# A planned attention and MLP kernel: new durations for the planner, and the order of its work searched anew

## The chip, the cores and the metric

The kernel runs on one core of one Trainium2 chip. The metric is the device time of one execution in microseconds, the median of three runs. Of a core's engines, five matter here: TensorE (PE in the profile, with its weight loads as a row of their own, PEld), VectorE (DVE), ScalarE (ACT), GpSimd (POOL), and SyncE (SP), which here only issues DMAs. Each engine works through its own instructions in a fixed order and waits at semaphores for the others.

## The reference

Four layers on one sequence of 2048 tokens of width 448, in bfloat16. An attention layer with 16 heads of 28 and an MLP with squared ReLU alternate twice, with the same weights both times.

```
def _A_ref(x, wqkv, wo):                 # H = 16, Dh = 28
    qkv = (x @ wqkv).reshape(B, S, 3, H, Dh) ...
    scores = jnp.einsum("bhqd,bhkd->bhqk", q, k) * Dh ** -0.5
    p = _softmax(scores, axis=-1)
    o = jnp.einsum("bhqk,bhkd->bhqd", p, v)
    return o.transpose(0, 2, 1, 3).reshape(B, S, D) @ wo

def _B_ref(x, w1, b1, w2, b2):           # F = 1792
    r = relu(x @ w1 + b1)
    return (r * r) @ w2 + b2

x = x + _A_ref(_layernorm(x), A_wqkv, A_wo)
x = x + _B_ref(_layernorm(x), B_w1, B_b1, B_w2, B_b2)
x = x + _A_ref(_layernorm(x), A_wqkv, A_wo)
x = x + _B_ref(_layernorm(x), B_w1, B_b1, B_w2, B_b2)
```

The softmax takes the exponential of 2 x 16 x 2048 x 2048 scores. Spread over 128 partitions this is 2048 units of 128x512 scores.

## The kernel before, in words

**Tiles.** The queries of a layer are cut into blocks of 256 (the last two of the second layer of 128), the heads into four groups of four, the keys into 16 blocks of 128. A *unit* is one head of one query block against as many key blocks as fill 128x512. TensorE computes scores as keys times queries with contraction over 32 rows, so that several heads run in different rows of the array side by side.

**Score groups.** `s_stream` takes three units at a time, the *score group*, into a tile `sc` of three PSUM banks; there are two such tiles. There are 683 groups. `e_stream` gives each group one exponential on ScalarE (L994), 1536 wide, into a tile `pt` (11 buffers). In some groups ScalarE takes only two of the units, 1024 wide, and VectorE the third: `a_unit` and `a_rest` compute its exponential in three VectorE passes (L1059 from PSUM, L1076, and L1090, which writes the result) and one GpSimd pass (L1083) between the last two. Which groups give a unit away is decided in `apart`: group numbers in `FORCE` do so, those in `SKIP` do not, and the others do it if VectorE's load and backlog in the plan are below limits (`BUSY`, `TB` and others).

**The other work.** `p_stream` multiplies the exponentials with the values (L1153, tile `oT`), which also gives the denominators. `norm_pair` and `norm_turn` divide. `chain` carries a query block through the output projection, the layer norm (statistics at L537 and L542, the inverse root on GpSimd, `xn` at L647, transposes on TensorE at L587, their copy `xnT` at L599), the MLP (matmuls at L684, ReLU at L1349 on VectorE or L1347 on ScalarE, square at L1356 or L1354, additions to `x` at L1289) and, in the first layer, the keys, values and queries of the second. All of this runs on TensorE and VectorE between the score groups. TensorE gets filler work as well: a score group can be computed several times over (up to `MORE` more times) and `heat` issues matmuls whose result nobody reads (L1407).

**The order.** There is no scheduler at run time. `Planner` simulates all engines while the kernel is built: every `Op` has an engine, a duration in microseconds, dependencies, and buffers to acquire; the planner repeatedly takes the operation that can start first (by priority where several can) and emits its instructions. `LAT` and `PAIR` are the delays that the plan assumes between the end of an operation on one engine and the start of one on another. `PACE` maps score-group numbers to settings of the planner's constants from there on. So a change of a duration or a constant changes no instruction's work, only which instructions are emitted (who computes a unit, filler) and their order on each engine.

Of the kernel before, what the change touches and what calls it, by code (L numbers as in the profile page):

```python
# [118 lines left out]
CUTS = (0, 10, 16)  # L119
CH = 4.0  # L120
QP = 8.0
FORCE = (26, 42, 46, 57, 59, 85, 86, 102, 105, 106, 107, 170, 171, 332, 335, 410, 413, 462, 466, 561, 563, 565, 567,
        576, 583, 584, 597, 598)
SKIP = (12, 13, 16, 18, 21, 22, 25, 29, 44, 47, 87, 151, 153, 154, 155, 168, 331, 333, 334, 372, 373, 375, 377, 412,
        559, 560, 562, 581, 595)
PACE = {
    0: {'ASIDE': 2.0, 'BUSY': 0.97, 'CH': 4.0, 'CHUNK': 1, 'C_PRIO': 1.6, 'EV': 2.9, 'FAR': 9, 'HOLD': 6,
         'KEEP': 6, 'L0N': 7.0, 'L1N': 5.6, 'LAG': 12, 'LASTP': 3.2, 'LEAD': 15, 'LOW': 0.85, 'MARGIN': 1.5,
         'MORE': 1, 'NEAR': 6, 'PRE': 0.5, 'QP': 8.0, 'SLACK': 0.5, 'SOON': 0, 'SPAN': 15, 'TB': 1.8, 'V_AGE':
         6, 'V_LAST': 1.8, 'V_LATE': 4.6, 'V_PRIO': 8.5, 'V_WAIT': 5},  # L130
    6: {'V_LATE': 3.5, 'C_PRIO': 2.6},
    12: {'HOLD': 4, 'KEEP': 2, 'V_LATE': 5.2},
    18: {'CHUNK': 3, 'V_LAST': 3},
    36: {'CHUNK': 2},
    54: {'QP': 5},
    60: {'V_AGE': 4},
    66: {'V_AGE': 5},
    84: {'BUSY': 0.995},
    90: {'NEAR': 8, 'BUSY': 0.97},
    96: {'NEAR': 6, 'BUSY': 0.995},  # L140
    114: {'NEAR': 8},
    150: {'LAG': 5, 'CH': 5, 'SOON': 0.5},
    156: {'MARGIN': 2.5, 'L0N': 6.0},
    162: {'TB': 2.2, 'KEEP': 5},
    174: {'KEEP': 2, 'HOLD': 5, 'LAG': 8},
    192: {'MORE': 2},
    198: {'MORE': 1, 'FAR': 12},
    204: {'NEAR': 6, 'EV': 1.5, 'PRE': -0.3},
    210: {'NEAR': 8, 'EV': 2.9, 'PRE': 0.5},
    216: {'KEEP': 3, 'V_WAIT': 3.5},  # L150
    240: {'LAG': 16, 'LASTP': 2.6, 'SPAN': 11},
    246: {'LAG': 8, 'LASTP': 3.2, 'SPAN': 15, 'MORE': 2, 'V_WAIT': 2.5},
    252: {'V_LATE': 4.0},
    282: {'MORE': 1},
    288: {'MORE': 2},
    306: {'CHUNK': 3},
    318: {'CHUNK': 2},
    360: {'ASIDE': 1.0, 'HOLD': 4},
    366: {'V_AGE': 3, 'L1N': 5.8},
    402: {'L1N': 5.0, 'CHUNK': 1, 'HOLD': 6},  # L160
    414: {'L1N': 5.8},
    426: {'HOLD': 5, 'SPAN': 20},
    432: {'LOW': 0.9},
    444: {'V_PRIO': 2.8},
    450: {'V_PRIO': 8.5},
    522: {'HOLD': 6, 'V_LATE': 4.6},
    528: {'HOLD': 5, 'V_LATE': 4.0},
    534: {'PRE': 0.8, 'L0N': 7.8, 'LOW': 0.95},
    540: {'ASIDE': 0.3, 'SPAN': 11},
    552: {'LAG': 5},  # L170
    576: {'FAR': 17},
    582: {'FAR': 12},
    588: {'FAR': 17, 'V_LAST': 3.5, 'SLACK': 0.2},
    594: {'V_LAST': 3, 'SLACK': 0.5},
    648: {'KEEP': 2, 'CHUNK': 2, 'LEAD': 12},
}


# [12 lines left out]
class Op:  # L191
    __slots__ = ("eng", "dur", "fn", "deps", "acq", "rel", "mode", "sets", "start", "end", "res", "turn", "ready", "lat", "need", "got", "more", "room", "port", "durs")

    def __init__(self, eng, dur, fn, deps=(), acq=None, rel=None, mode="full", sets=(), lat=0.0, need=1, port=False):
# [7 lines left out]
        self.need, self.got, self.more, self.port = need, [], 0.0, port  # L202


LAT = {"PE": 0.25, "ACT": 0.28, "DVE": 0.07, "POOL": 0.10, "DMA": 2.0, "-": 0.0}
PAIR = {("PE", "ACT"): 0.275, ("PE", "DVE"): 0.197, ("DVE", "ACT"): 0.1, ("DVE", "POOL"): 0.1, ("DVE", "DVE"): 0.035,
        ("POOL", "DVE"): 0.035, ("PE", "PE"): 0.0, ("ACT", "ACT"): 0.0, ("POOL", "POOL"): 0.0}


# [99 lines left out]
def kernel(  # L309
# [593 lines left out]
    def s_stream():  # L903
        while at[0] < len(units):
            gi = len(gbuf)
            globals().update(PACE.get(gi, {}))
            js = ahead(3)
            us = [units[j] for j in js]
            gbuf.append({"n": len(us)})

            def fn(e, gi=gi, us=us, js=js):
                sc = ps_sc.tile([P, 3 * 512], DT.float32, name="sc", tag="sc")
                gbuf[gi]["sc"] = sc
                dst = [sc[:, k * 512:k * 512 + 512] for k in range(len(us))]
                ks = list(range(len(us)))

                def next_at(j):
                    at[0] = j
                    rest = ahead(1)
                    at[0] = rest[0] if rest else len(units)  # L920
                    return rest
                own, j = True, None
                if OWN3 and bank_free(o.start) and next_at(js[-1] + 1):
                    j = apart(at[0], o.start, us)
                if j is None and len(us) == 3 and THIRD:
                    own = False
                    next_at(js[1] + 1)
                    j = apart(at[0], o.start, us[:2], 0.0)
                if j is None:
                    next_at(js[-1] + 1)  # L930
                else:
                    if not own:
                        us, ks = us[:2], ks[:2]
                        gbuf[gi]["n"] = 2
                    us, ks = us + [units[j]], ks + [3]
                    taken.add(j)
                    gbuf[gi]["in"] = not own and units[j][0] == us[0][0]
                    held[0] += not gbuf[gi]["in"]
# [12 lines left out]
                for k, (pi, kb, r, hh) in zip(ks, us):  # L951
                    where.setdefault((pi, kb), []).append((gi, k, hh))
                    if len(where[pi, kb]) == G:
                        pl.tok["u", pi, kb] = o

                short = (HOT if len(units) - at[0] > ENDU else HOTE) - pl.load(HWIN)
                again = 0
                if short > 0 and gi > 0:
                    last = ("e" in gbuf[gi - 1] and gbuf[gi - 1]["e"].end) or pl.clock["ACT"] + 1.35
                    again = max(0, min(MORE, int(min(o.room, last - LAT["PE"] - 0.05 - o.end) / 0.22)))  # L960
                o.more = 0.22 * again
                for i in list(range(4)) * (again + 1):
                    for k, (pi, kb, r, hh) in enumerate(us):
                        if i >= r:
                            continue
                        l, qb, g, *_ = passes[pi]
                        t0, nt = blocks[l][qb]
                        rows = slice(DHP * hh, DHP * hh + DHP)
                        nc.tensor.matmul(dst[k][:, i * nt * P:(i + 1) * nt * P],  # L969
                                         lhsT=K_sb[l][rows, g, (kb + i) * P:(kb + i + 1) * P],  # L970
                                         rhs=Q_sb[rows, g, t0 * P:(t0 + nt) * P],
                                         start=True, stop=True, tile_position=(DHP * hh, 0))
            o = gbuf[gi]["s"] = Op("PE", 0.227, fn,
                                   deps=list({d for u in us for d in needs(u)}), acq=R_sc, mode="row", sets=("s", gi))
            yield o
        s_left.clear()
        pl.tok["send"] = o
# [7 lines left out]
    def e_stream():  # L985
        gi = 0
        while gi < len(gbuf) or s_left:
            yield Op("-", 0.0, None, deps=[("s", gi)])
            n = gbuf[gi]["n"] * 512

            def fn(e, gi=gi, n=n):
                e_now[:] = [e_now[0] + n // 512 + ("x" in gbuf[gi]), gi]
                pt = gbuf[gi]["pt"] = ptp.tile([P, 3 * 512], DT.bfloat16, name="pt")
                t = nc.scalar.activation(out=pt[:, 0:n], in_=gbuf[gi]["sc"][:, 0:n], func=AF.Exp,  # L994
                                         scale=float(np.log(2.0)) * 2.0 ** -FRAC)
                if gbuf[gi].get("x") is gbuf[gi]["s"]:
                    apart_from(gi, t)
            o = gbuf[gi]["e"] = Op("ACT", n / 1200 + 0.051, fn, deps=[("s", gi)], acq=R_pt, need=n // 512 + gbuf[gi].get("in", 0),
                                   rel=gbuf[gi]["s"], sets=("e", gi))
            yield o  # L1000
            gi += 1
# [456 lines left out]
```

## Time and profile before

| | |
|---|---|
| median of three runs | 845.28 us (845.02 to 845.38) |
| the profiled execution's own time | 845.39 us |
| span of its trace | 843.3 us |
| busy PE / DVE / ACT / POOL | 805.7 / 788.5 / 827.2 / 210.3 us |
| exponentials on ScalarE, 1536 and 1024 wide | 445 and 238 |
| units on VectorE (L1059) | 237 |
| score matmuls (L969) | 5120 |
| filler matmuls of `heat` (L1407) | 133 |
| granted TensorE clock | 1.000 |

The busy time of an engine is the union of its instructions' intervals. Instructions of one engine overlap (the next one starts before the last has written its result), so the mean time of one instruction is longer than the step from one to the next.

### The profile page before, as it was taken

How to read it: one execution, taken by the hardware profiler on the slowest of the kernel's cores; microseconds unless marked ns; L12 is line 12 of the kernel's file. 1: busy time of each engine (PE TensorE's matmuls, PEld its weight loads, DVE VectorE, ACT ScalarE, POOL GpSimd, SP SyncE). 2: the span in 40 equal slices, each digit the busy share in tenths (PEclk: the TensorE clock that was granted, in tenths of full speed). 3: DMA queues.
4: the chain of work that ended last, by engine and by line, in shares of the span. 5: the costliest groups of instructions: out<-in, count | busy, mean ns of one | idle time of the engine just before them, and what ended most of it. 6: DMA issues, size and time to landing. Idle time of an engine off the chain costs nothing.

```text
span 843.3 us, 28075 instructions
## 1 busy us (share of the span) xinstructions
PE 805.7 (96%) x12089; PEld 422.3 (50%) x12089; DVE 788.5 (93%) x1531; ACT 827.2 (98%) x698; POOL 210.3 (25%) x332
## 2 busy tenths in 40 slices
PE   8999999999999999999999999999999999999997
PEld 4455544454544545455445444434455454545665
DVE  7999999999999999999999999999999998989954
ACT  8999999999999999999999999999999999999994
POOL 3211322322222223322222223322212223121200
PEclk9999999999999999999999999999999999999999
DMA  9200100000000000000000000011100001000000
GB/s 244 74 3 2 26 22 12 15 15 16 8 9 16 15 15 16 15 3 15 2 3 2 2 2 3 15 29 29 32 9 14 26 15 31 21 13 15 14 20 13
DMA packets 32312, 17.94 MB, mean 21 GB/s; under 512 B 17786, under 2 KB 31739, under 8 KB 32188
## 3 DMA queue, kind: packets, MB, share of 16 engines
q1 hardware_dynamic: 32188, 16.16, 7.0%
q8 instruction: 94, 1.54, 0.8%
q14 instruction: 30, 0.25, 0.1%
HBM read 13.87 MB, written 2.06 MB: 19 GB/s over the span
## 4 chain that ended last, share of the span: by engine, by line
ACT 43%; PE 33%; DVE 15%; issue 8%; POOL 1%; DMA 0%; ACTq 0%; DVEq 0%; POOLq 0%
ACT pt L994 43%; PE mt L684 13%; PE sc L969 11%; PE oT L1153 6%; DVE r L1349 2%; DVE v_i L1059 2%; DVE v_e L1076 1%; DVE pt L1090 1%; PE mt L1407 1%; PE sc L684 1%; PE tp L587 1%; DVE K_sb L1076 1%; DVE st L537 1%; DVE x_sb L1289 1%; DVE K_sb L1059 1%
## 5 line engine op out<-in xcount | busy, mean ns | idle before, releaser
L994 ACT ACTIVATE pt<-sc 128x1536 bf16<-128x1536 f32 (+1 forms) x683 | 816.9, 1464 | 1.7 <-PE sc L969 1.4
L969 PE MATMUL sc<-Q_sb,K_sb 32*128 32x256 bf16 (+1 forms) x5120 | 301.0, 265 | 27.7 <-ACT pt L994 20.7
L969 PEld LDWEIGHTS <-K_sb 32*128 32x128 bf16 x5120 | 128.6, 92 | 209.1 <-issue 160.7
L1083 POOL TENSOR_SCALAR v_i<-v_i 128x512 int32<-128x512 int16 x126 | 89.2, 708 | 291.8 <-DVE v_e L1076 290.2
L1153 PE MATMUL oT<-pt,V_sb 128*32 128x256 bf16 (+1 forms) x4098 | 157.0, 268 | 0.8 <-ACT pt L994 0.5
L684 PE MATMUL mt<-xnT,w 128*128 128x256 bf16 (+1 forms) x928 | 121.9, 269 | 0.6 <-DVE r L1349 0.3
L1153 PEld LDWEIGHTS <-V_sb 128*32 128x32 bf16 x4352 | 89.3, 96 | 52.9 <-issue 49.6
L684 PEld LDWEIGHTS <-w 128*128 128x128 bf16 x952 | 77.6, 98 | 36.4 <-issue 28.6
L1059 DVE TENSOR_SCALAR v_i<-sc 128x512 int32<-128x512 f32 x126 | 85.7, 682 | 5.2 <-PE sc L969 4.5
L1076 DVE SCALAR_TENSOR_TENSOR v_e<-v_i 128x512 f32<-128x512 uint16 x126 | 87.6, 699 | 0.3
L1083 POOL TENSOR_SCALAR K_sb<-K_sb 128x512 int32<-128x512 int16 x64 | 45.3, 708 | 138.6 <-DVE K_sb L1076 134.5
L1349 DVE TENSOR_SCALAR r<-mt 128x512 bf16<-128x512 f32 x108 | 73.7, 682 | 5.4 <-PE mt L684 4.7
L684 PE MATMUL mt<-w,V_sb 128*128 128x448 bf16 (+1 forms) x274 | 68.3, 352 | 0.0
L1083 POOL TENSOR_SCALAR V_sb<-V_sb 128x512 int32<-128x512 int16 x47 | 34.3, 729 | 101.6 <-DVE V_sb L1076 100.7
L1059 DVE TENSOR_SCALAR K_sb<-sc 128x512 int32<-128x512 f32 x64 | 43.7, 683 | 1.9 <-PE sc L969 1.6
L1289 DVE TENSOR_TENSOR x_sb<-x_sb,mt 128x448 bf16<-128x448 bf16 (+1 forms) x61 | 37.0, 607 | 8.9 <-PE mt L684 8.5
L1407 PE MATMUL mt<-xn,ident 128*128 128x448 bf16 x133 | 44.2, 355 | 1.1 <-DVE x_sb L1289 0.3
L1076 DVE SCALAR_TENSOR_TENSOR K_sb<-K_sb 128x512 f32<-128x512 uint16 x64 | 44.1, 694 | 0.1
L1090 DVE SCALAR_TENSOR_TENSOR pt<-v_e,v_i 128x512 bf16<-128x512 f32 x59 | 40.0, 679 | 3.8 <-POOL v_i L1083 3.8
L537 DVE BATCH_NORM_STATS2 st<-x_sb 128x6 f32<-128x448 bf16 x62 | 37.7, 611 | 0.8 <-DMA x_sb<-in_A_x_dram 0.6
L684 PEld LDWEIGHTS <-V_sb 128*128 128x128 bf16 x302 | 24.1, 98 | 25.1 <-issue 12.6
L1059 DVE TENSOR_SCALAR V_sb<-sc 128x512 int32<-128x512 f32 x47 | 31.9, 681 | 1.2 <-PE sc L969 1.0
(115 smaller groups left out, 828.0 us busy)
## 6 DMA issues: line engine op xcount, KB each, us to landing
rec<-scr SPq DMA_DIRECT2D x54, 128.0 KB
x_sb<-in_A_x_dram SPq DMA_DIRECT2D x8, 224.0 KB
out_dram<-x_sb SPq DMA_DIRECT2D x15, 112.0 KB
w<-in_B_w_dram SPq DMA_DIRECT2D x1, 1568.0 KB
w<-in_B_w_dram SPq DMA_DIRECT2D x1, 1344.0 KB
dn<-oT_sb SPq DMA_DIRECT2D x54, 4.0 KB
V_sb<-in_A_wqkv_dram SPq DMA_DIRECT2D x4, 168.0 KB
scr<-dn SPq DMA_DIRECT2D x27, 8.0 KB
```

The costliest lines, as they stand in the source:

```text
L537: nc.vector.bn_stats(out=box["st"][:, :], in_=x_sb[:, t0 + j, :] if src is None else src())
L684: nc.tensor.matmul(box["t"][:, c0:c0 + n], lhsT=lhsT() if callable(lhsT) else lhsT, rhs=rhs, start=a, stop=b)
L969: nc.tensor.matmul(dst[k][:, i * nt * P:(i + 1) * nt * P], lhsT=K_sb[l][rows, g, (kb + i) * P:(kb + i + 1) * P], rhs=Q_sb[rows, g, t0 * P: ...
L994: t = nc.scalar.activation(out=pt[:, 0:n], in_=gbuf[gi]["sc"][:, 0:n], func=AF.Exp, scale=float(np.log(2.0)) * 2.0 ** -FRAC)
L1059: t = nc.vector.tensor_scalar(out=box["i"], in0=two(src), scalar1=EXP_BIAS, scalar2=EXP_LOW, op0=ALU.add, op1=ALU.max)
L1076: nc.vector.scalar_tensor_tensor(out=box["h"], in0=box["f"], scalar=lin, in1=box["f"], op0=ALU.add, op1=ALU.mult)
L1083: (nc.vector if e == "DVE" else nc.gpsimd).tensor_scalar(out=box["e"], in0=box["n"], scalar1=2.0 ** 22, scalar2=EXP_BASE, op0=ALU.mult, op ...
L1090: nc.vector.scalar_tensor_tensor(out=box["two"](pd), in0=box["h"], scalar=low, in1=box["e"].bitcast(DT.float32), op0=ALU.add, op1=ALU.mult)
L1153: nc.tensor.matmul(box["t"][DHP * hh:DHP * hh + DHP, 0:n], lhsT=V_sb[l][:, kb + i, 4 * g + hh, :], rhs=p[:, c0:c0 + n], start=begin and kb ...
L1289: nc.vector.tensor_tensor(out=x_sb[:, tb, lo:hi], in0=x_sb[:, tb, lo:hi], in1=t[:, 0:hi - lo], op=ALU.add)
L1349: nc.vector.tensor_scalar(out=r[:, 0:w], in0=t[:, 0:w], scalar1=0.0, scalar2=None, op0=ALU.max)
L1407: nc.tensor.matmul(t[:, 0:D], lhsT=ident[:, :], rhs=xns[0][:, 0:D], start=True, stop=True)
```

## The change

It sets five figures of the planner: a score group on TensorE from 0.227 to 0.234 us, the fixed part of an exponential from 0.051 to 0.0555 us, the delay after ScalarE from 0.28 to 0.30, that from TensorE to VectorE from 0.197 to 0.200, and that from VectorE to GpSimd from 0.10 to 0.15. The tables `FORCE`, `SKIP` and `PACE` are replaced by others. No function is added.

```
-FORCE = (26, 42, 46, 57, 59, 85, 86, 102, 105, 106, 107, 170, ...
-SKIP = (12, 13, 16, 18, 21, 22, 25, 29, 44, 47, 87, 151, ...
+FORCE = (72, 73, 106, 109, 145, 146, 167, 177, 179, 180, 181, 189, ...
+SKIP = (74, 77, 79, 89, 91, 92, 93, 94, 95, 105, 144, 147, ...
 PACE = {
-    0: {'ASIDE': 2.0, 'BUSY': 0.97, 'CH': 4.0, 'CHUNK': 1, ... 'MORE': 1, ...
-    192: {'MORE': 2},
-    198: {'MORE': 1, 'FAR': 12},
-    246: {'LAG': 8, 'LASTP': 3.2, 'SPAN': 15, 'MORE': 2, 'V_WAIT': 2.5},
-    282: {'MORE': 1},
-    288: {'MORE': 2},
+    0: {'ASIDE': 2.0, 'BUSY': 0.97, 'CH': 4.0, 'CHUNK': 3, ... 'MORE': 1, ...
+    536: {'TB2': 2.2, 'EPRIO': 8, 'MORE': 3},
+    544: {'EPRIO': 2.5, 'MORE': 1, 'NEAR': 2},
 ...
-LAT = {"PE": 0.25, "ACT": 0.28, "DVE": 0.07, "POOL": 0.10, "DMA": 2.0, "-": 0.0}
-PAIR = {("PE", "ACT"): 0.275, ("PE", "DVE"): 0.197, ("DVE", "ACT"): 0.1, ("DVE", "POOL"): 0.1, ...
+LAT = {"PE": 0.25, "ACT": 0.3, "DVE": 0.07, "POOL": 0.10, "DMA": 2.0, "-": 0.0}
+PAIR = {("PE", "ACT"): 0.275, ("PE", "DVE"): 0.2, ("DVE", "ACT"): 0.1, ("DVE", "POOL"): 0.15, ...
 ...
-            o = gbuf[gi]["s"] = Op("PE", 0.227, fn,
+            o = gbuf[gi]["s"] = Op("PE", 0.234, fn,
 ...
-            o = gbuf[gi]["e"] = Op("ACT", n / 1200 + 0.051, fn, ...
+            o = gbuf[gi]["e"] = Op("ACT", n / 1200 + 0.0555, fn, ...
```

Lines of the changed kernel are numbered 7 lower than those of the kernel before from the planner on (L994 becomes L987).

More of the change, by code (lines that the diff above doesn't have):

```diff
@@ L121 @@
 QP = 8.0
[L122 to L125, printed above, removed]
-PACE = {
[L127 to L145, printed above, removed]
-    192: {'MORE': 2},
-    198: {'MORE': 1, 'FAR': 12},
[L148 to L151, printed above, removed]
-    246: {'LAG': 8, 'LASTP': 3.2, 'SPAN': 15, 'MORE': 2, 'V_WAIT': 2.5},
-    252: {'V_LATE': 4.0},
-    282: {'MORE': 1},
-    288: {'MORE': 2},
[L156 to L175, printed above, removed]
@@ new lines @@
+FORCE = (72, 73, 106, 109, 145, 146, 167, 177, 179, 180, 181, 189, 199, 209, 212, 249, 252, 262, 275, 277, 278, 279,
+        299, 388, 391, 465, 466, 467, 471, 490, 491, 492, 493, 523, 525, 528, 534, 535, 539, 554, 558, 612, 613, 632,
+        633, 638, 646, 647, 653, 655)
+SKIP = (74, 77, 79, 89, 91, 92, 93, 94, 95, 105, 144, 147, 148, 150, 178, 183, 184, 188, 190, 197, 213, 216, 217, 220,
+        222, 223, 248, 250, 254, 256, 257, 258, 273, 274, 276, 301, 341, 342, 464, 468, 470, 489, 522, 526, 527, 530,
+        608, 616, 617, 622, 624, 625, 631, 635, 636, 639, 640, 645, 650, 651, 652)
@@ new lines @@
+PACE = {
+    0: {'ASIDE': 2.0, 'BUSY': 0.97, 'CH': 4.0, 'CHUNK': 3, 'C_PRIO': 1.6, 'EPRIO': 2.5, 'EV': 2.9, 'FAR': 9,
+         'HOLD': 5, 'KEEP': 6, 'L0N': 7.4, 'L1N': 5.6, 'LAG': 12, 'LASTP': 3.2, 'MARGIN': 1.5, 'MORE': 1,
+         'NEAR': 6, 'SOON': 0, 'TB': 2.2, 'TB2': 0.9, 'V_AGE': 6, 'V_PAST': 2, 'V_PRIO': 8.5},
+    8: {'EV': 2.2},
+    16: {'CH': 5, 'MARGIN': -1},
+    32: {'V_AGE': 5},
+    80: {'CHUNK': 2},
+    104: {'LAG': 5},
+    112: {'LAG': 12, 'SOON': 1.0, 'BUSY': 1.01},
+    120: {'KEEP': 2},
+    168: {'TB': 2.6},
+    192: {'TB': 1.8},
+    224: {'LAG': 8},
+    240: {'V_AGE': 6},
+    248: {'LAG': 12},
+    256: {'LAG': 8},
+    280: {'V_PAST': 0, 'L1N': 5.0},
+    296: {'V_PRIO': 3.5, 'LAG': 16},
+    304: {'V_PRIO': 8.5, 'LAG': 8},
+    352: {'V_PAST': 2},
+    360: {'CH': 3.3},
+    376: {'ASIDE': 1.0, 'C_PRIO': 5.5},
+    384: {'ASIDE': 2.0, 'C_PRIO': 1.6, 'LAG': 16},
+    392: {'LAG': 8},
+    408: {'FAR': 17, 'ASIDE': 0.6},
+    448: {'C_PRIO': 3.2},
+    456: {'C_PRIO': 1.6, 'TB2': 2.2, 'LAG': 12},
+    480: {'NEAR': 8},
+    528: {'TB2': 0.5},
+    536: {'TB2': 2.2, 'EPRIO': 8, 'MORE': 3},
+    544: {'EPRIO': 2.5, 'MORE': 1, 'NEAR': 2},
+    552: {'NEAR': 8},
+    568: {'FAR': 12},
+    584: {'EV': 1.5},
+    592: {'EV': 2.2},
+    624: {'V_PRIO': 3.5, 'SOON': 0.5, 'LASTP': 2.6},
+    632: {'V_PRIO': 8.5, 'SOON': 1.0, 'LAG': 16},
+    648: {'HOLD': 3, 'NEAR': 2},
+    664: {'CHUNK': 1},
+    672: {'CHUNK': 2},
@@ L202, in __init__ @@
         self.need, self.got, self.more, self.port = need, [], 0.0, port
-LAT = {"PE": 0.25, "ACT": 0.28, "DVE": 0.07, "POOL": 0.10, "DMA": 2.0, "-": 0.0}
-PAIR = {("PE", "ACT"): 0.275, ("PE", "DVE"): 0.197, ("DVE", "ACT"): 0.1, ("DVE", "POOL"): 0.1, ("DVE", "DVE"): 0.035,
+LAT = {"PE": 0.25, "ACT": 0.3, "DVE": 0.07, "POOL": 0.10, "DMA": 2.0, "-": 0.0}
+PAIR = {("PE", "ACT"): 0.275, ("PE", "DVE"): 0.2, ("DVE", "ACT"): 0.1, ("DVE", "POOL"): 0.15, ("DVE", "DVE"): 0.035,
         ("POOL", "DVE"): 0.035, ("PE", "PE"): 0.0, ("ACT", "ACT"): 0.0, ("POOL", "POOL"): 0.0}
@@ L997, in fn @@
                     apart_from(gi, t)
-            o = gbuf[gi]["e"] = Op("ACT", n / 1200 + 0.051, fn, deps=[("s", gi)], acq=R_pt, need=n // 512 + gbuf[gi].get("in", 0),
+            o = gbuf[gi]["e"] = Op("ACT", n / 1200 + 0.0555, fn, deps=[("s", gi)], acq=R_pt, need=n // 512 + gbuf[gi].get("in", 0),
                                    rel=gbuf[gi]["s"], sets=("e", gi))
```

## The prediction

> **What bounds the kernel now.** I read the page's busy shares first, then ScalarE in order of time, then the two forms of its exponential, then stretches of 100 us, and last the end of the kernel in order of time. The page (busy us, share, instructions):
>
> ```profile
> PE 805.7 (96%) x12089; PEld 422.3 (50%) x12089; DVE 788.5 (93%) x1531; ACT 827.2 (98%) x698; POOL 210.3 (25%) x332
> ```
>
> ScalarE in order of time (start, length; equal instructions merged; in brackets the idle time before and who ended it):
>
> ```profile
> 10.78 10.92 ACT L994 ACTIVATE pt<-sc 128x1536 bf16<-128x1536 f32 x8 [0.61 <-PE sc L969]
> 22.45 806.34 ACT L994 ACTIVATE pt<-sc 128x1536 bf16<-128x1536 f32 x675 [0.75 <-PE sc L969]
> 830.09 0.38 ACT L1347 ACTIVATE r<-mt 128x256 bf16<-128x256 f32 x1 [1.31 <-PE mt L684]
> ```
>
> So the span of 843.3 us has three parts: 10.8 us before the first exponential, 818.0 us of exponentials (10.78 to 22.45 + 806.34 = 828.79) with one hole of 0.75 us, and 14.5 us after the last. ScalarE is the bound of the middle part. Its two forms, groups of costs kept apart by shape:
>
> ```profile
> L994 ACT ACTIVATE pt<-sc 128x1536 bf16<-128x1536 f32 x445 | 649.5, 1611 | 1.7 <-PE sc L969 1.4
> L994 ACT ACTIVATE pt<-sc 128x1024 bf16<-128x1024 f32 x238 | 270.2, 1190 | 0.0
> ```
>
> A unit that VectorE takes saves ScalarE 1611 - 1190 = 0.421 us. The means contain overlap; from start to start the trace has 1.345 and 0.920 us on average (445 and 238 of them make up the 818 us), and 1.330 and 0.903 at the least. The difference to the least, 10.6 us over all 682 steps, is what the exponentials started late: 39 steps are late by over 60 ns and hold 6.9 us, the rest are a few ns each. The next view shows why VectorE does not take more units (busy us in each stretch: PE, PEld, DVE, ACT, POOL, then the granted clock):
>
> ```profile
> 500.00:600.00 100.00, 93.77 (x1383) 45.67 (x1380) 97.54 (x184) 100.00 (x86) 30.52 (x45) 1.00 0.07 19
> 600.00:700.00 100.00, 97.14 (x1410) 50.20 (x1408) 98.26 (x186) 100.00 (x86) 25.37 (x38) 1.00 0.07 19
> 700.00:800.00 100.00, 96.66 (x1611) 50.95 (x1609) 90.61 (x172) 100.00 (x85) 21.27 (x33) 1.00 0.07 19
> ```
>
> VectorE is nearly as full as ScalarE, except from 700 us on. The clock stays at 1.00 even where TensorE is busy 94%.
>
> **The change, part by part.** Durations in the planner change nothing on the chip by themselves; what does is the new order. I counted the instructions of both programs and where they stand.
>
> *Units.* The wide exponentials go from 445 to 440 and the narrow ones from 238 to 243; L1059 goes from 237 to 242. ScalarE loses 5 x 0.421 = **2.1 us**, on the path.
>
> *What VectorE pays.* Five units are 15 passes. One follows another after 0.60 us where it waits for nothing (their mean of 0.68 to 0.70 us contains overlap), so 9.0 us; two 512-wide squares (0.33 us each from start to start) move to ScalarE at the end, and small shifts bring the sum to +8.1 us. In groups of 40 score groups, three of the five land in groups 600 to 639 (about 725 to 774 us), the stretch with 90.61 above. With the trace's step for every form, VectorE's work in groups 560 to 639 is 84.1 of ScalarE's 94.9 us before and 89.6 of 93.6 after: its free part falls from 10.8 to 4.0 us. The fullest stretch of 40 is at 98% after (99% before), so VectorE bounds none. Price on the path: nothing, covered by ScalarE. If that cover were gone it would be up to 8.1 us. GpSimd's five more passes (0.71 us each) lie in its 75% of idle time.
>
> *What TensorE gets.* 234 of the 256-wide score matmuls fall away (repeats: `MORE` is 1 nearly everywhere, it was 2 from group 288 on and in some earlier stretches) and 12 of 128 come. Six 256-wide ones take some 0.22 us side by side: -8.6 + 0.2 us. `heat` issues 16 more at 0.19 us: +3.0 us. Net -5.3 us, off the path. Between consecutive score groups, counting 0.22 us for six score matmuls, the steps of the others and 0.1 us at each change of array mode, 51 intervals before hold over 0.3 us more than their exponential, 38 after. Sorting the late starts by this backlog, they are as frequent at 0 to 0.3 us of backlog as at 0.3 to 0.5. So I give nothing for it; it bears on the range.
>
> *The head.* The instruction orders are the same up to the eighth score group. There, at 21.70 us, ScalarE idles 0.75 us because this runs before the ninth:
>
> ```profile
> 20.72 1.04 PE L684 MATMUL mt<-xnT,wq 128*128 128x256 bf16 x8
> 22.01 0.61 PE L969 MATMUL sc<-Q_sb,K_sb 32*128 32x256 bf16 x12 [0.25 <-DVE K_sb L707]
> ```
>
> The new order puts four more of these matmuls (0.11 us each) ahead of the score group. Their bank is freed by the same copy at L707, so they do not fit into the 0.25 us: **+0.44 us**. The second longest late start, 0.40 us at 38.9 us (group 21, 1.6 us of other matmuls in one interval), has no such interval in the new order: **-0.40 us**.
>
> *The end.* The last exponential is 1024 wide in both. Before, it ends at 828.78, and this follows (start, length; DVE and PE only):
>
> ```profile
> 830.46 0.29 DVE L1238 TENSOR_TENSOR oTn<-oT,rec 128x128 bf16<-128x128 f32 x1
> 830.81 0.36 PE L684 MATMUL sc<-wo,oTn 128*128 128x448 bf16 x1 [0.76 <-DVE oTn L1238]
> 831.21 0.63 DVE L537 BATCH_NORM_STATS2 st<-sc 128x6 f32<-128x448 f32 x1 [0.46 <-PE sc L684]
> 831.39 2.24 PE L684 MATMUL sc<-w,V_sb 128*128 128x448 bf16 x11
> 831.88 0.18 DVE L542 BATCH_NORM_AGGREGATE mv<-st 128x2 f32<-128x6 f32 x1
> 833.00 0.40 DVE L647 TENSOR_SCALAR xn<-x_sb,mv,rstd 128x448 bf16<-128x448 bf16 x1 [0.43 <-POOL rstd L565]
> 833.47 0.39 PE L587 MATMUL tp<-ident,xn 128*128 128x128 bf16 x4
> 833.69 0.73 PE L684 MATMUL sc<-w,V_sb 128*128 128x448 bf16 x3
> 833.89 0.42 DVE L599 COPY xnT<-tp 128x512 bf16<-128x512 bf16 x1 [0.49 <-PE tp L587]
> 834.46 0.62 DVE L1289 TENSOR_TENSOR x_sb<-x_sb,sc 128x448 bf16<-128x448 bf16 x1
> ```
>
> The new order leaves more of the second to last block's MLP behind the last exponential: 24 hidden-layer matmuls of 128 columns instead of 8. Before the last `wo` matmul stand 22 of these; with 0.056 us each they end at about 830.86, where that matmul started before: +0.05. Then VectorE has a ReLU of 256 columns (0.33 us) between statistics and their aggregation; the aggregation waits 0.67 us for the statistics anyway, of which the ReLU overlaps all but **0.20**. On TensorE all 15 second-layer matmuls (0.19 each, 2.84 us) stand ahead of the last block's transposes, where 12 stood before. They start at about 831.16 and end at 834.00, so the transposes go from 833.47 to 834.00 (in this the 0.25 are contained). On VectorE the addition to `x` (L1289), now ahead of the copy `xnT`, waits for the last of them until 834.20 and takes 0.53: the copy starts at 834.73 instead of 833.89, **+0.84 us**. Behind it the orders are the same. The lower bound is 0 (the block's idle time of 4.54 us on ScalarE before 835.46 shows slack, but not on this chain), the upper 1.2, if the ReLU and squares on ScalarE come 0.4 later.
>
> *Late starts.* The other 37 late steps hold 6.9 - 0.88 - 0.40 = 5.6 us. The order is new, so none of these need recur and others will appear. What can be counted is alike: units whose score bank VectorE reads only after the next score group is issued, 23 before and 18 after; `pt` buffers released by the group just ahead of their reuse, 20 and 15. I take 5.6 again, between 2.8 and 8.4.
>
> *Sum.* -2.1 + 0.44 - 0.40 + 0.84 = -1.2 us. The profiled execution took 845.39 us, 2.1 more than its span and 0.1 above the median, so 845.28 - 1.2 = **844.0 us**, with late starts at their ends 841.2 to 846.8.
>
> **The rivals.** (1) *The late starts go as well.* The five new figures lie nearer to this trace (the mean step 1.345 is longer than the old 1280 + 51 = 1.331), so a plan made with them may meet fewer surprises. For it: 51 to 38 and 23 to 18. Against it: late starts do not follow the backlog. If a third of the 5.6 us goes, 844.0 - 1.9 = 842.1 us.
>
> (2) *VectorE is late in groups 560 to 639*, the other side. With 4.0 us free instead of 10.8, the read of the third bank (L1059) comes late, the next score group waits for the bank, and ScalarE for it. The waits of the score groups' weight loads for L1059 hold 5.6 us before (15 times); doubling them all on the path gives 849.6, half of that 846.8. It decides against the kernel from 3.0 us of new late starts on, which makes 847.0. Against it: at 98% in 600 to 700 us ScalarE lost under 2 us.
>
> (3) *The clock falls.* Fewer repeats leave TensorE with more small pauses. The first matmuls of the trace, 448 wide, follow each other after 0.373 us, later ones after 0.189, so a slow state exists. Filled to 0.93, TensorE at half speed would lose 0.86 us for each us of it; 4 us of it give 847.4. Against it: 1.00 in all stretches, at 93.77 busy too, and with `MORE` at 1 in the first 190 groups. The Trainium skill, TensorE: Matmul & The Clock Gate, Part 1, says that an idle window of about 3.4 us brings the half clock, and under its second failure mode that frequent short pauses can do so too. By the first rule nothing happens here, as no TensorE pause in the trace is over 0.8 us; by the second this rival would come true. The trace agrees with the first.
>
> **How the numbers follow.** Forecast 0.46 (own range 843.0 to 845.4), rival 1 0.33, rival 2 0.17, rival 3 0.04. A measurement of this kernel can tell about 0.2%, 1.7 us: faster means below 843.6, slower above 847.0. Of the forecast 0.12 lies below 843.6 and 0.34 within; of rival 1 0.30 below and 0.03 within; of rival 2 0.03 within and 0.14 above; rival 3 is above. Faster 0.42, same 0.40, slower 0.18. The range of 8 in 10 runs from 841.6 (rival 1 with half of the late starts gone and a little more of the end hidden) to 847.0.
>
> **What would show it.** Units: 440 and 243 exponentials, with a start-to-start sum some 2.1 us shorter. Head: a hole of about 1.2 us before the ninth exponential and none over 0.3 us near 39 us. End: about 15.3 us from the end of the last exponential to the end of the span, with L1289 ahead of the last `xnT`. Late starts: ScalarE's time from first to last exponential beyond the two steps. The prediction is wrong if that part moves by over 2 us, if VectorE's releases of `sc` show in ScalarE's or TensorE's idle time in 680 to 775 us, or if 448-wide matmuls after 10 us are 0.37 us apart.

## The result, and the profile after

The kernel after takes 843.84 us (median of 17 runs, 843.60 to 845.57). The kernel before, over 17 runs, takes 845.14 us (844.87 to 846.76). The ratio is 0.9982, with a 95% interval of 0.9975 to 0.9989: 1.3 us less, just inside the 0.2% that the prediction had called "same". Forecast were 844.0 us. (Two of the 17 runs of the kernel after and four of the kernel before are some 1.7 us longer than the others, which leaves the medians where they are.)

The profiled execution took 843.81 us, with a span of 842.03 us. The page's line of engines (busy us, share, instructions):

```profile
PE 794.8 (94%) x11883; PEld 419.9 (50%) x11883; DVE 791.7 (94%) x1544; ACT 826.4 (98%) x700; POOL 215.9 (26%) x337
```

ScalarE in order of time:

```profile
10.54 10.94 ACT L987 ACTIVATE pt<-sc 128x1536 bf16<-128x1536 f32 x8 [0.61 <-PE sc L962]
22.41 213.21 ACT L987 ACTIVATE pt<-sc 128x1536 bf16<-128x1536 f32 x178 [0.93 <-PE sc L962]
235.96 590.72 ACT L987 ACTIVATE pt<-sc 128x1536 bf16<-128x1536 f32 x497 [0.33 <-PE sc L962]
826.44 0.74 ACT L1347 ACTIVATE V_sb<-r 128x512 bf16<-128x512 bf16 x1
```

The exponentials still run without a large hole, now with two that the view can show after the start: 0.93 us before the ninth and 0.33 us at 236 us. (A line of 497 instructions contains others whose idle time the merging leaves out because the next instruction starts before the last has ended.) The two forms:

```profile
L987 ACT ACTIVATE pt<-sc 128x1536 bf16<-128x1536 f32 x440 | 647.1, 1617 | 1.9 <-PE sc L962 1.9
L987 ACT ACTIVATE pt<-sc 128x1024 bf16<-128x1024 f32 x243 | 278.8, 1197 | 0.0
```

Cut at the first exponential's start and the last one's end, the span comes apart like this. "Least" is the sum over all exponentials of the shortest step of each form (1.330 and 0.904 us); "late" is what the steps hold beyond it.

| us | before | after | difference |
|---|---|---|---|
| ahead of the first exponential | 10.78 | 10.54 | -0.24 |
| exponentials, all | 818.01 | 816.14 | -1.87 |
| of these: least | 807.00 | 804.87 | -2.13 |
| of these: late starts (the rest are the last one's length and rounding) | 10.57 | 10.91 | +0.34 |
| behind the last exponential | 14.52 | 15.36 | +0.83 |
| span | 843.31 | 842.03 | -1.27 |

So the five units were gained in full, and the late starts and the end took some half of it back. A late start is named below by the time at which the late exponential starts. VectorE holds the five units where it had room (busy us of PE, PEld, DVE, ACT, POOL, then the clock):

```profile
500.00:600.00 100.00, 90.85 (x1373) 45.10 (x1365) 98.33 (x187) 100.00 (x88) 28.37 (x43) 1.00 0.07 19
600.00:700.00 100.00, 96.09 (x1363) 48.62 (x1359) 97.23 (x184) 100.00 (x86) 29.45 (x40) 1.00 0.07 20
700.00:800.00 100.00, 96.14 (x1652) 52.77 (x1653) 95.92 (x186) 100.00 (x86) 24.73 (x36) 1.00 0.07 19
```

From 700 to 800 us it went from 90.61 to 95.92 and ScalarE stayed at 100.00. The late starts of groups 560 to 639 sum to 1.1 us before and after.

The end in order of time (PE and DVE; the last exponential ends at 826.68):

```profile
828.57 0.35 PE L677 MATMUL sc<-wo,oTn 128*128 128x448 bf16 x1
828.96 0.63 DVE L530 BATCH_NORM_STATS2 st<-sc 128x6 f32<-128x448 f32 x1 [0.49 <-PE sc L677]
829.05 2.81 PE L677 MATMUL mt<-w,V_sb 128*128 128x448 bf16 x14
829.50 0.41 DVE L1342 TENSOR_SCALAR r<-mt 128x256 bf16<-128x256 f32 x1
829.83 0.17 DVE L535 BATCH_NORM_AGGREGATE mv<-st 128x2 f32<-128x6 f32 x1
830.94 0.40 DVE L640 TENSOR_SCALAR xn<-x_sb,mv,rstd 128x448 bf16<-128x448 bf16 x1 [0.43 <-POOL rstd L558]
831.70 0.39 PE L580 MATMUL tp<-ident,xn 128*128 128x128 bf16 x4
831.90 0.62 DVE L1282 TENSOR_TENSOR x_sb<-x_sb,mt 128x448 bf16<-128x448 bf16 x1 [0.57 <-PE mt L677]
832.44 0.42 DVE L592 COPY xnT<-tp 128x512 bf16<-128x512 bf16 x1
832.91 1.95 PE L677 MATMUL sc<-xnT,w 128*128 128x128 bf16 x32 [0.82 <-DVE xnT L592]
```

The sequence is the forecast one: the ReLU (L1342) stands between statistics and aggregation, 15 second-layer matmuls stand ahead of the transposes (the one at 828.87 belongs to them), and the addition (L1282) ahead of the copy `xnT` (L592).

### The profile page after: what moved, and what is told of

The parts are those of the page before. It is cut to its first block, busy times and chain, and to the rows that moved or that the text cites. A ratio compares the mean times of both kernels' runs of the same rounds, so it can differ in the third digit from the quotient of the medians.

```text
span 842.0 us, 27672 instructions
## 1 busy us (share of the span) xinstructions
PE 794.8 (94%) x11883; PEld 419.9 (50%) x11883; DVE 791.7 (94%) x1544; ACT 826.4 (98%) x700; POOL 215.9 (26%) x337
## 4 chain that ended last, share of the span: by engine, by line
ACT 42%; PE 30%; DVE 19%; issue 8%; POOL 1%; DMA 0%; ACTq 0%; DVEq 0%; POOLq 0%
ACT pt L987 42%; PE mt L677 12%; PE sc L962 10%; PE oT L1146 6%; DVE v_i L1052 2%; DVE v_e L1069 2%; DVE pt L1083 2%; DVE r L1342 2%; DVE x_sb L1282 1%; PE mt L1400 1%; DVE st L530 1%; PE sc L677 1%; DVE K_sb L1083 1%; DVE V_sb L1069 1%; DVE V_sb L1052 1%
## 5 line engine op out<-in xcount | busy, mean ns | idle before, releaser
L987 ACT ACTIVATE pt<-sc 128x1536 bf16<-128x1536 f32 (+1 forms) x683 | 814.9, 1468 | 1.9 <-PE sc L962 1.9
L962 PE MATMUL sc<-Q_sb,K_sb 32*128 32x256 bf16 (+1 forms) x4898 | 292.3, 265 | 34.1 <-ACT pt L987 28.2
L962 PEld LDWEIGHTS <-K_sb 32*128 32x128 bf16 x4898 | 121.3, 92 | 214.4 <-issue 166.2
L1076 POOL TENSOR_SCALAR v_i<-v_i 128x512 int32<-128x512 int16 x130 | 92.8, 714 | 258.0 <-DVE v_e L1069 255.8
L1146 PE MATMUL oT<-pt,V_sb 128*32 128x256 bf16 (+1 forms) x4064 | 151.3, 268 | 1.0 <-DVE K_sb L592 0.8
L1052 DVE TENSOR_SCALAR v_i<-sc 128x512 int32<-128x512 f32 x130 | 88.9, 684 | 4.2 <-PE sc L962 3.4
L1069 DVE SCALAR_TENSOR_TENSOR v_e<-v_i 128x512 f32<-128x512 uint16 x130 | 89.2, 693 | 0.5
L1342 DVE TENSOR_SCALAR r<-mt 128x512 bf16<-128x512 f32 (+1 forms) x109 | 74.1, 680 | 7.5 <-PE mt L677 7.2
L677 PE MATMUL mt<-w,V_sb 128*128 128x448 bf16 x274 | 67.8, 355 | 0.0
L1400 PE MATMUL mt<-xn,ident 128*128 128x448 bf16 x149 | 48.5, 356 | 1.0 <-DVE oT_sb L1172 0.5
L1052 DVE TENSOR_SCALAR K_sb<-sc 128x512 int32<-128x512 f32 x67 | 45.7, 685 | 3.1 <-PE sc L962 2.9
L1069 DVE SCALAR_TENSOR_TENSOR K_sb<-K_sb 128x512 f32<-128x512 uint16 x67 | 46.0, 692 | 0.2
L1282 DVE TENSOR_TENSOR x_sb<-x_sb,mt 128x448 bf16<-128x448 bf16 x61 | 37.3, 612 | 3.7 <-PE mt L677 3.5
L557 POOL TENSOR_TENSOR ve<-mv,eps_t 128x2 f32<-128x2 f32 (+1 forms) x34 | 14.1, 415 | 93.8 <-DVE mv L535 93.2
```

Of the source, the lines that this page charges most:

```text
L677: nc.tensor.matmul(box["t"][:, c0:c0 + n], lhsT=lhsT() if callable(lhsT) else lhsT, rhs=rhs, start=a, stop=b)
L962: nc.tensor.matmul(dst[k][:, i * nt * P:(i + 1) * nt * P], lhsT=K_sb[l][rows, g, (kb + i) * P:(kb + i + 1) * P], rhs=Q_sb[rows, g, t0 * P: ...
L1052: t = nc.vector.tensor_scalar(out=box["i"], in0=two(src), scalar1=EXP_BIAS, scalar2=EXP_LOW, op0=ALU.add, op1=ALU.max)
L1069: nc.vector.scalar_tensor_tensor(out=box["h"], in0=box["f"], scalar=lin, in1=box["f"], op0=ALU.add, op1=ALU.mult)
L1076: (nc.vector if e == "DVE" else nc.gpsimd).tensor_scalar(out=box["e"], in0=box["n"], scalar1=2.0 ** 22, scalar2=EXP_BASE, op0=ALU.mult, op ...
L1146: nc.tensor.matmul(box["t"][DHP * hh:DHP * hh + DHP, 0:n], lhsT=V_sb[l][:, kb + i, 4 * g + hh, :], rhs=p[:, c0:c0 + n], start=begin and kb ...
```

## The experiments

The theory under test: the time is the sum of what ScalarE's exponentials take, with 0.42 us for each unit, and of late starts and an end that the order sets one by one. Rivals: VectorE was the bound in the stretch that took the units; the late starts follow from bad figures and go with good ones; the filler is worth nothing. Each kernel is the kernel after with one edit (the figures alone are an edit of the kernel before). Ratios are to the kernel before, whose median was 845.03 to 845.13 us in these rounds.

### The tables without the figures, the figures without the tables

```
# the tables alone
-LAT = {"PE": 0.25, "ACT": 0.3, ...          ("PE", "DVE"): 0.2, ... ("DVE", "POOL"): 0.15
+LAT = {"PE": 0.25, "ACT": 0.28, ...         ("PE", "DVE"): 0.197, ... ("DVE", "POOL"): 0.1
-  Op("PE", 0.234, fn, ...     Op("ACT", n / 1200 + 0.0555, fn, ...
+  Op("PE", 0.227, fn, ...     Op("ACT", n / 1200 + 0.051, fn, ...
# the figures alone: FORCE, SKIP, PACE of the kernel before
```

> The new tables with the five old planner figures. Its order has 236 units on VectorE (446 wide exponentials), and leaves the second to last block's last 15 second-layer matmuls behind everything else. By the sum of units and end: +0.4 us for one unit fewer than before (237), and about +3.5 us at the end (15 matmuls of 0.19 us, addition and store), so about 849.0 us, with a middle part of about 818.4 us. If the gain came from the tables as such, it keeps most of the 1.3 us: about 843.9.

> The five new planner figures with the old tables. 241 units (441 wide exponentials), and the same long end as with the tables alone. By the sum: -1.7 us in the middle (about 816.4 us) and about +3.5 at the end, so about 847.0 us. If figures nearer to the trace cure late starts, the middle is shorter than 815 us: late starts fall from 10.6 us to under 8.

Tables alone: 856.71 us, ratio 1.0134 (1.0119 to 1.0149). Figures alone: 869.68 us, ratio 1.029 (1.0274 to 1.0307). Both expectations were far too low. In both the units hardly matter (236 and 241 of them). Late starts hold 16.5 and 31.9 us instead of 10.9, and the end takes 19.9 us instead of 15.4. About two thirds of what the late starts hold beyond the 10.9 us is one late exponential at the change of layers, 3.5 us late at 534.5 us with the tables alone and 14.1 us at 544.8 us with the figures alone. With the figures alone (PE, then ACT, in order of time):

```profile
539.25 0.76 PE L587 MATMUL tp<-ident,xn 128*128 128x128 bf16 x8 [3.08 <-DVE xn L647]
540.79 1.87 PE L684 MATMUL mt<-xnT,wk 128*128 128x256 bf16 x8 [0.78 <-DVE xnT L599]
542.45 1.70 PE L684 MATMUL mt<-wv,xnT 128*128 128x448 bf16 x4
544.08 1.04 PE L969 MATMUL sc<-Q_sb,K_sb 32*128 32x256 bf16 x12
```

```profile
544.79 1.94 ACT L994 ACTIVATE pt<-sc 128x1024 bf16<-128x1024 f32 x2 [13.95 <-PE sc L969]
```

The second layer's score groups need the keys of a first-layer block whose chain comes late, and ScalarE stands still for 13.95 us. So the tables fit only the figures under which they were searched; each half of the change costs 12 or 25 us, the whole of it gains 1.3.

### Six units less

From group 600 to 647 a unit is given to VectorE in every third group at most.

```
+        gi = len(gbuf) - 1
+        if 600 <= gi < 648 and gi % 3:
+            return None
```

> The changed kernel with units allowed in only every third group from 600 to 647: 236 units instead of 242, six of them gone from that stretch, the order before it unchanged. By the sum each costs 0.42 us on ScalarE, so +2.5 us, and an end that is 0.2 shorter (copy ahead of the addition): about 846.1 us. If VectorE was late in that stretch (the rival on VectorE), part of the 2.5 comes back as fewer late starts: under 845.5 us.

846.34 us, ratio 1.0013 (1.0004 to 1.0023), 446 and 237 exponentials. From first to last exponential it takes 818.71 us, 2.57 more than the kernel after, for six units: 0.43 each. The late starts are 10.85 us, as in the kernel after (10.91). So the units are worth the whole of their 0.42 us. Taking VectorE's load in that stretch away again does not make late starts fewer: it was not late there.

### More work for VectorE in groups 560 to 639

L1069 squares a unit's polynomial. It is issued twice, in nine of that stretch's units or in all 31; the second result overwrites the first with the same values.

```
-            nc.vector.scalar_tensor_tensor(out=box["h"], ...
+            for _ in range(2 if 560 <= gi < 640 and gi % 3 == 0 else 1):
+                nc.vector.scalar_tensor_tensor(out=box["h"], ...
```

> The changed kernel with one VectorE pass (the square of a unit, same data, same result) done twice in 9 of the 31 units of groups 560 to 639, unplanned: 9 x 0.60 = 5.4 us more work where the count left VectorE 4.0 us free. If VectorE's room is real and waits are soaked up by the buffers, +1.4 us at most: 843.8 to 845.2. If each pass is on the path, +5.4: 849.2.

> As the kernel with nine extra passes, but in all 31 units of groups 560 to 639: 18.6 us of extra VectorE work. By the count 18.6 - 4.0 = 14.6 us come onto the path, less what the free quarter of VectorE in groups 640 to 680 takes up later (up to 10 us): between +5 and +15, 849 to 858. If VectorE has no room at all, +18.6: 862.

Nine more passes (5.4 us): 847.37 us, ratio 1.0027 (1.0016 to 1.0037), between the two times expected. First to last exponential is 819.58, +3.44. Thirty-one (18.6 us): 864.52 us, ratio 1.0232 (1.0217 to 1.0247), above both times expected; 836.80 from first to last, +20.7, more than the passes themselves (the clock fell to half twice, for 3.41 us each). The free part of 4.0 us that was counted for VectorE here took up only 2.0 of the 5.4 us, since the room is not where a pass comes late: a late read of a score bank holds up the next score group. With nine, the late starts in these groups go from 1.08 to 4.58 us, and the waits of score groups (weight loads and matmuls) for L1052, VectorE's read of the third bank, from 1.8 us (678 to 772 us) to 8.4 (678 to 776 us). The longest late start, 0.97 us at 738.03 us, follows such a wait:

```profile
737.32 0.61 PE L962 MATMUL sc<-Q_sb,K_sb 32*128 32x256 bf16 x12 [1.33 <-DVE K_sb L1052]
```

This is the mechanism of the prediction's second rival, and it is real; the change stopped short of it. The extra passes were not in the plan, so this prices work that comes unplanned. Another late start, 0.76 us at 694.96 us, comes from a filler matmul that waits for VectorE's ReLU.

### The filler left out

The repeats of score groups (L955) and the matmuls of `heat` (L1398) are not issued. Neither has a result that is read, and the order of all else is the same.

```
-                for i in list(range(4)) * (again + 1):
+                for i in range(4):
...
-                t = bank(o, "mt")
-                for _ in range(k):
-                    nc.tensor.matmul(t[:, 0:D], lhsT=ident[:, :], ...
+                bank(o, "mt")
```

> The changed kernel with every filler matmul left out and the order otherwise kept: 546 repeated score matmuls and 149 of heat are gone, some 48 us of TensorE's work; the warm-up at the start stays. If the clock needs them, the granted clock falls below 1.00 in stretches, 256-wide matmuls come 0.21 us apart instead of 0.11, and the time rises above 847. If TensorE's own work keeps the clock up, granted clock 1.00 and 843.8 us, or 0.2 to 0.5 less because score groups start earlier.

853.42 us, ratio 1.0103 (1.0084 to 1.0121). All of the loss lies between first and last exponential (825.51, +9.4), where late starts grow from 10.9 to 20.3 us. The trace records when the granted clock changed: between 120 and 585 us it fell to half seven times, for 54.6 us in all. The 46 exponentials that start in these seven stretches, or up to 1.5 us behind them, hold 10.7 us more of late starts than in the kernel after, and all others together 1.4 us less, so the loss is the clock's. Two of the falls, each with the 3.41 us ahead of it, columns as above:

```profile
119.25:122.66 3.41, 1.64 (x29) 0.88 (x25) 3.41 (x7) 3.41 (x4) 1.49 (x3) 1.00 0.02 1
122.66:126.07 3.41, 3.41 (x24) 1.70 (x19) 2.77 (x6) 3.09 (x3) 0.41 (x1) 0.50 0.07 10
542.50:545.91 3.41, 2.09 (x42) 1.11 (x40) 3.38 (x7) 3.41 (x4) 1.54 (x2) 1.00 0.03 6
545.91:569.80 23.89, 19.23 (x236) 6.86 (x229) 21.79 (x40) 22.44 (x20) 7.47 (x10) 0.50 0.11 26
```

TensorE is busy 1.64 of 3.41 us ahead of the first fall and 2.09 of 3.41 us ahead of the second. In the slow stretches 256-wide matmuls follow each other after 213 ns instead of 109, and ScalarE waits for the score groups (22.44 of 23.89 us busy). The longest pause of TensorE in the whole of the middle is 0.95 us. So the clock falls without any long pause, after a short time with many short ones.

### The layer norm's block at the end

```
-    648: {'HOLD': 3, 'NEAR': 2},
+    648: {'HOLD': 3},
```

From score group 648 on, other work is let in nearer to the next exponential's start (`NEAR` 8, as from 552 on, instead of 2). The middle part keeps its length.

> The changed kernel with one setting taken out from score group 648 on (NEAR 2), which puts the last block's transposes ahead of 7 of the 15 second-layer matmuls and the copy xnT ahead of the addition to x. Units stay at 242. If the end's loss of 0.65 us to the copy lies on that chain, the time from the last exponential to the end falls from 15.36 to about 14.8 us (0.1 to 0.2 is given back by 7 matmuls that stand behind the transposes): about 843.3 us. If the end is set by something else, 843.8.

843.68 us (843.59 to 845.29, 10 runs), ratio 0.9983 (0.9974 to 0.9993). The end takes 15.15 us, 0.21 less instead of the 0.56 expected. Its last chain is earlier by what was meant (last exponential's end: 826.73):

```profile
831.39 0.39 PE L580 MATMUL sc<-ident,xn 128*128 128x128 bf16 x4
831.81 0.43 DVE L592 COPY xnT<-sc 128x512 bf16<-128x512 bf16 x1 [0.55 <-PE sc L580]
...
832.37 1.06 PE L677 MATMUL sc<-xnT,w 128*128 128x128 bf16 x16
...
835.50 0.73 PE L677 MATMUL mt<-w,V_sb 128*128 128x448 bf16 x3
```

The copy comes 5.08 us after the last exponential instead of 5.76, which is 0.68 earlier. But three second-layer matmuls of the block before now stand between the last block's hidden and second layer (835.50), and TensorE has no pause from 827.25 us on. What the chain gains, the matmuls still to be done take back: VectorE's last addition starts only 0.03 us earlier after the last exponential. The other 0.18 us of the gain lie behind that addition (see the term *End* of the sum below).

### Units at the very end

`STOP` keeps VectorE from taking any of the last 80 units; here, any of the last 20.

```
-STOP = 80
+STOP = 20
```

> The changed kernel with units allowed until 20 units before the end instead of 80: 249 units, seven more, all after group 640 where VectorE is free a quarter of the time. ScalarE gains 7 x 0.42 = 2.9 us; but the order leaves two hidden-layer tiles and 15 second-layer matmuls more of the second to last block behind the last exponential. By their steps the end grows by about 3.5 us: about 844.4. If the end's extra work is hidden in the last block's chain, 841.0.

849.76 us, ratio 1.0053 (1.0036 to 1.007), with 433 and 250 exponentials. The middle is 813.15 us, -2.98, as forecast for seven units. The end is 24.23 us, +8.9 where 3.5 were expected. TensorE there:

```profile
831.08 2.81 PE L677 MATMUL mt<-w,V_sb 128*128 128x448 bf16 x14
833.72 0.39 PE L677 MATMUL sc<-xnT,w 128*128 128x128 bf16 x4
833.95 1.73 PE L677 MATMUL mt<-xnT,w 128*128 128x128 bf16 x28
835.51 1.95 PE L677 MATMUL sc<-xnT,w 128*128 128x128 bf16 x32
```

VectorE's units took the place of the MLP of the blocks before, which is still to be done when the exponentials are over. Units are cheap only while something else still covers what VectorE puts off.

### Late starts moved one by one

TensorE gets the same instructions, but the few matmuls ahead of a late score group are issued just behind it; in one kernel for the three longest late starts (the ninth exponential and those at 236 and 442 us), in the other for eleven more places, with the setting of the end from above.

```
+                self.count += e == "PE"
+                if e == "PE" and self.count in LATER:
+                    self.kept = o.fn
+                else:
+                    o.fn(e)
+                    if self.kept and ("s" in [d[0] for d in o.sets]):
+                        self.kept, f = None, self.kept
+                        f(e)
```

> The changed kernel with three pieces of other TensorE work issued behind instead of ahead of a score group: the four query matmuls ahead of the ninth group, and the four matmuls ahead of groups 186 and 359, where exponentials start 1.06, 0.53 and 0.37 us late; nothing else in the order differs. If late starts come from in-order work ahead of the score group, these three fall to about 0.6, 0.1 and 0.1: 1.2 us less, 842.6. If the moved work is late for somebody else, new late starts behind them give it back: 843.8.

> As the kernel with three pieces moved, with eleven more of the late groups (72, 93, 140, 156, 204, 215, 256, 302, 376, 652, 679, together 1.75 us late) and the end of the run e3_end. By the sum -1.2 for the three, -1.2 for two thirds of the others and -0.2 for the end: 841.2. If only the three large ones can be cured this way, 842.4.

Three moved: 843.82 us (843.76 to 844.02), ratio 0.998 (0.9971 to 0.9989). The middle is 816.09 us, 0.05 less instead of 1.2. Fourteen moved: 844.00 us, ratio 0.9987 (0.9977 to 0.9997). Its profiled execution took 844.82 us, and its middle is 0.97 us longer; but there the clock fell to half from 390.26 to 393.67 us (the last section shows it), and the four groups that it held up are 1.24 us later than in the kernel after. Without them the middle would be 0.27 us shorter, where 2.4 us less were expected. With three moved, ScalarE at the start reads:

```profile
10.79 10.95 ACT L996 ACTIVATE pt<-sc 128x1536 bf16<-128x1536 f32 x8 [0.61 <-PE sc L971]
22.16 6.82 ACT L996 ACTIVATE pt<-sc 128x1536 bf16<-128x1536 f32 x5 [0.43 <-PE sc L971]
29.21 1.45 ACT L996 ACTIVATE pt<-sc 128x1536 bf16<-128x1536 f32 x1 [0.22 <-PE sc L971]
```

and TensorE:

```profile
21.72 0.40 PE L971 MATMUL sc<-Q_sb,K_sb 32*128 32x256 bf16 x6
22.05 0.61 PE L686 MATMUL mt<-xnT,wq 128*128 128x256 bf16 x4
22.59 0.39 PE L971 MATMUL sc<-Q_sb,K_sb 32*128 32x256 bf16 x6
```

The ninth exponential is late by 0.55 us instead of 1.06, and a later one by 0.35 that was on time before, another by 0.18. At 236 us 0.53 becomes 0.15, and the next step goes from 0.02 to 0.24; at 442 us 0.37 becomes 0.01, and the next 0.04 to 0.40. TensorE is behind by the same work wherever it stands; the late start moves by one to seven groups.

No kernel here clearly beats the kernel after: 843.68 and 843.82 against 843.84 us are not told apart by these runs.

## Why the prediction was right, and where it was not

The sum was -1.2 us, the medians differ by -1.3 and the spans of the two profiled executions by -1.27. That the total is so close is in part luck: the late start at the head came out 0.26 us below its term and the first exponential 0.24 us early for a reason outside the sum, while the other late starts grew by 0.56 us. The forecast of 844.0 us is rounded, too: 845.28 - 1.2 is 844.1. The terms one by one:

*Units, -2.1.* Right: the least sum fell by 2.13, and six units less gave 2.57 back, seven more took 2.98.

*Head, +0.44.* Mis-sized: the late start before the ninth exponential grew from 0.875 to 1.059 us, +0.18. The step that failed was that the four more matmuls do not fit into the 0.25 us in which TensorE waited, because their bank is freed by the same copy. They ran there without a gap (columns: start, length, PE and DVE merged):

```profile
19.61 1.05 PE L677 MATMUL mt<-xnT,wk 128*128 128x256 bf16 x8
20.50 1.54 PE L677 MATMUL mt<-xnT,wq 128*128 128x256 bf16 x12
20.70 0.69 DVE L700 CAST K_sb<-mt 128x512 bf16<-128x512 f32 x1
21.97 0.61 PE L962 MATMUL sc<-Q_sb,K_sb 32*128 32x256 bf16 x12
```

The copy (L700, before L707) started 10.16 us after the first exponential's start, before 21.27 - 10.78 = 10.49. It ended at 21.39, when the first eight of the matmuls were through (20.50 + 8 x 0.11 = 21.38), and the other four followed at once. The score group starts at 21.97, 11.43 us after the first exponential's start, before 11.23.

*Group 21, -0.40.* Right: this late start, of the exponential at 40.6 us, goes from 0.404 to 0.

*End, +0.84.* The total is +0.83, and partly by luck. Right were its first two steps (no real change up to the last `wo` matmul, which started 0.14 us earlier where 0.05 later was forecast; +0.20 for the aggregation, 0.67 to 0.87 after the statistics). The transposes came +0.33 later after the last exponential instead of +0.53, and the copy `xnT` +0.65 instead of +0.84, both for the most part from that earlier `wo` matmul. The missing 0.19 us came back behind VectorE's last addition, from whose start to the end of the span 2.73 us became 2.92. The store is not longer: it has landed 1.76 us after that start before, and 1.77 us after. What comes later is ScalarE's last closing instruction (DRAIN), 2.56 instead of 2.29 us after it. The four experiments that keep this order of the end (no filler, nine and thirty-one extra passes, three moved) have the 2.92 us as well, and the three in which the copy `xnT` (L592) stands ahead of the addition (L1282) as it did before (six units less, the setting of the end, fourteen moved) have the 2.74 of before. So it goes with the order of the end and is a cost that the prediction did not list; why ScalarE closes later was not settled.

*Other late starts, 0 in the sum (5.6 us again).* They grew by 0.56 us, inside the range of 2.8 to 8.4 and against rival 1. New ones are 0.53 us at 236.0 us, ahead of which TensorE's second-layer matmuls waited for a copy on VectorE (L1172), and 0.37 at 442.0 us with key matmuls behind the same kind of copy. The count over 60 ns is alike (38 to 39 before, 39 to 40 after). Better figures did not make fewer late starts. The moved score groups show that single pieces do not remove them; why their sum stays near 11 us over such different orders (10.6, 10.9, 10.9 without six units) was not settled.

*What the sum had not.* The first exponential started 0.24 us earlier in an order that is the same up to there. The four transposes at 6.5 us take 0.40 instead of 0.61 us, before and after:

```profile
6.50 0.61 PE L587 MATMUL sc<-ident,xn 128*128 128x128 bf16 x4 [0.23 <-DVE xn L647]
6.47 0.40 PE L580 MATMUL sc<-ident,xn 128*128 128x128 bf16 x4 [0.45 <-DVE xn L640]
```

The trace of before records the full clock from 7.07 us on. The kernel with three moved score groups, in the order of the kernel after, records it from 7.07 us on too, takes 0.61 us for these transposes and starts its first exponential at 10.79 us. The six experiments that record it from 4.55 to 6.61 us on start at 10.54 to 10.58. So this is when the clock became full in one execution, not the change. Without it the profiled difference would have been -1.0.

*VectorE, +8.1 at no cost.* Right as to the cost: ScalarE lost nothing in that stretch (late starts of 1.1 us before and after). The cover was thinner than its 4.0 us, since of 5.4 us more 3.4 came through. VectorE's busy time rose by 3.2 us only, while the sum of its instructions' lengths rose by 9.5; the difference is overlap. Rival 2 was priced too low: its 5.6 us in 15 waits are those for the tile `v_i` alone, and with the tiles `V_sb` and `K_sb`, which L1059 writes too, the weight loads wait 10.4 us in 31 waits. After, it is 11.2 us in 35, so these waits hardly grew, in keeping with a price of nothing.

*TensorE, -5.3 at no cost.* Right in this kernel: in its profiled execution 256-wide matmuls that stand side by side follow each other after 109 to 120 ns throughout the middle. But the margin became smaller: the least busy 3.41 us between 15 and 825 us are 77% busy before and 60% after, and at 60% the clock fell in the profiled execution of the kernel with fourteen moved groups. And the ground given for rival 3's low chance was wrong. Of the two rules of the Trainium skill, TensorE: Matmul & The Clock Gate, that the prediction set against each other, it said that the trace agrees with the first, the idle window of about 3.4 us in Part 1. The kernel without filler had no pause over 0.95 us, and its clock was 0.50 for 23.89 us on end. That is what the Trainium skill, in the same page, describes of another kernel under "A second HAM failure mode: psum-queue depth-cycling": frequent short pauses. The trace of before could not have told the two apart: it has no such pause and no 3.41 us under 77% busy.

## What to carry to other kernels

Where one engine is busy 98% and the order is fixed ahead, price a change as units on that engine times the step saved (0.42 us here, confirmed with five, six and seven of them), and price the start and end separately from the timeline. Free time that is counted over a long stretch of the second engine is worth only part of itself to work that the plan did not place (2.0 of 4.0 us here), late starts that come from too much work in a place move when a piece of that work is moved, and figures and tables that were searched together are one change, not two. Filler matmuls can be worth 1% through the clock, so ask what they do, and how empty the emptiest 3.41 us would be without them, before calling TensorE's time free.

## What the runs showed of the hardware

In these traces the granted clock is full or half, and it changes in steps of 3.41 us: it was half for 3.41, 6.83, 10.24 or 23.89 us. Of the twelve falls between 4 and 825 us in all profiles, each came behind 3.41 us in which TensorE was busy 15 to 61%. Ten of the traces can be cut into such pieces of 3.41 us from their first record of the full clock on, some 2400 pieces in all. Up to 54% busy the clock fell behind each, from 55 to 61% behind some, and above that behind none. It came back only behind a piece that was at least 98% busy; pieces of 64 to 95% did not bring it back. The busy share of a longer stretch does not tell: without the filler, 15 us with 13.00 us busy ended in a fall at 518.61 us, and 765 to 780 us with 12.17 us busy in none.

Where the pieces lie differs from one execution to the next. The same matmuls at 387 us, in the kernel with fourteen moved groups (first two lines) and in the kernel after:

```profile
386.85:390.26 3.41, 2.04 (x29) 0.95 (x27) 3.41 (x9) 3.41 (x4) 0.62 (x1) 1.00 0.01 2
390.26:393.67 3.41, 3.35 (x18) 0.65 (x13) 2.55 (x7) 3.41 (x3) 0.62 (x1) 0.50 0.00 0
386.85:390.26 3.41, 2.04 (x31) 0.87 (x27) 3.41 (x9) 3.41 (x4) 0.62 (x1) 1.00 0.01 2
390.26:393.67 3.41, 3.32 (x28) 1.13 (x27) 3.31 (x8) 3.41 (x4) 0.62 (x1) 1.00 0.00 0
```

TensorE is busy 2.04 us in both, and the clock fell in one. Whether a piece of the kernel after began just there is not known, as its trace has no record of the clock in it.

The same happens at the start. In the profiled execution of the kernel with six units less, the clock was full from 4.37 us on, and half again from 7.78 us on, behind a piece with 1.78 of 3.41 us busy:

```profile
7.78:11.20 3.42, 3.42 (x19) 2.44 (x17) 1.95 (x5) 1.12 (x2) 0.00 (x0) 0.50 1.02 315
```

```profile
8.82 1.91 PE L677 MATMUL mt<-xnT,wq 128*128 128x256 bf16 x8
10.53 1.37 PE L677 MATMUL mt<-xnT,wk 128*128 128x256 bf16 x8
```

and the first wide matmuls of the kernel after:

```profile
8.26 1.04 PE L677 MATMUL mt<-xnT,wq 128*128 128x256 bf16 x8
9.13 1.04 PE L677 MATMUL mt<-xnT,wk 128*128 128x256 bf16 x8
```

The eight matmuls took 1.91 instead of 1.04 us, and the first exponential started at 12.27 instead of 10.54 us. So where such a piece begins can cost 1.7 us here, more than the whole change gained.
